# Routing cut into sixteen one-instruction steps, with a new emission order for attention, early table and early weights

## The chip, the cores and the metric

The kernel runs on one NeuronCore of a Trainium2 chip. The metric is the device time of one execution in microseconds (us). Several executions are timed and their median counts. One further execution is recorded by the profiler, and all rows shown here are of that one.

## The reference, cut to what matters

Attention over 8 batches, 8 heads, 576 positions and 64 features is the sum of two parts: one on queries, keys and values averaged over groups of 4, and one in a band of |i-j| < 4. Each token's 8 heads are joined to a row of 512, and the 4608 rows go through a mixture of 8 experts, one expert for each token.

```python
q_d = q.reshape(B, H, Sd, 4, D).mean(axis=3)      # k_d, v_d the same
out_up = np.repeat(sm_attn(q_d, k_d, v_d), 4, axis=2)
scores = np.where(abs(i - j) < 4, scale * q @ k.T, -1e9)
attn = np.exp(scores - scores.max(-1)); attn /= attn.sum(-1) + 1e-9
x = (out_up + attn @ v)  ->  [4608, 512]
...
logits = x @ w_gate + modality_bias[modality_id]
e_idx = np.argmax(logits, axis=1)
gate_w = softmax(logits)[token, e_idx]
for e in range(8):
    h = np.maximum(x[e_idx == e] @ w1[e], 0.0)
    out[e_idx == e] = gate_w[e_idx == e, None] * (h @ w2[e])
```

## The kernel before, in words

**Attention.** The work is cut into 32 units n of two heads each, four units to a batch b. TensorE (PE) transposes q and k (`tp`, `tpt`), multiplies the band in tiles of 24 queries by 32 keys (`sc`, L375) and the averaged part (`scd`, L401). ScalarE (ACT) copies the transposes out (`kT`, `qT`), takes the exponentials of the band (`le`, L392) and of the averaged part (`de`, L414, three to a unit), and copies `Pw`, `PdT`, `vd` and `Od`. VectorE (DVE) takes the maxima (`lm`, `dm`), subtracts (`le`, L387), sums (`z`), inverts (`zr`), transposes (`lt`, L439) and adds both parts to `X` (L490). GpSimd (POOL) averages q (`qe`, `qd`) and divides `le` (L428) and `de` (L432) by their sums. PE then multiplies by v (`avd` L468, `avl` L483). SyncE (SP) issues the loads of q, k and v, the stores of x to the table `xs`, and the weight loads (L851, L854); each of these is one entry in one queue.

**Order.** The order is not left to a scheduler in this part. `PHASE` gives each step a time: step s of unit n is due at n + PHASE[s] (plus ODD[s] for odd n), a routing step of batch b at 4b + PHASE[s]. Further calls with times of their own (loads, early table, early weights) are put on the same list, the list is sorted, and the instructions are emitted in that order. Every engine runs its own instructions in the order of emission, and waits at the first one whose data is not there. So the table decides only who stands behind whom.

**Routing.** For each of the first 6 batches, while attention of later batches runs: PE forms the logits (`lg`, `lgt`), ACT copies them (`LT`), DVE sums them (`L`, L545), adds the bias, finds the maximum and subtracts it (`ch1`, L552 to L555), finds the expert (`ch2`, L566 to L576, `oh` and the running count `acc`), ACT takes the exponential (`ex`, L559), DVE forms the gate (`gt`), PE the place in the expert's list (`pr`, L591 to L595), DVE the slot (`pl`, L603 to L607), and POOL scatters pairs of token and gate to the table `tab` (`st`, L642, up to 5 to a batch). The last two batches are routed after attention.

**Early table and early units.** After 4 batches the counts per expert are taken (`cp`, L654, one PE matmul) and some 25 short DVE instructions (`first`, L657 to L767) find an expert that already has 1024 tokens. Its first 1024 are two early units of 512: SP reads their entries (`tg`), POOL gathers their rows (`xg`, L937, four gathers for the first), SP loads the weights in chunks c (`wload`) and POOL and DVE split each chunk into a high part (CAST, L876) and a low part, raw minus high (`H<-raw`, L882: `wsplit`). The experts' layers (L1005, L1061) follow attention: the early units, then three large units of 1024 tokens and small ones for the rest.

Of the kernel before, what the change touches and what calls it, by code (L numbers as in the profile page):

```python
# [7 lines left out]
F32 = mybir.dt.float32  # L8
# [30 lines left out]
EB = 4  # L39
# [34 lines left out]
}  # L74

ODD = {"Od": 0.0089, "PdT1": 0.0014, "X0": 0.0451, "avd": 0.0124, "avl0": -0.0606, "avl1": -0.068, "de2": 0.0109, "dm": -0.0066, "exp": -0.0422, "kT0": 0.0073, "kT2": -0.0188, "le1": -0.0126, "lm1": -0.0049, "nd": 0.1052, "nl": 0.1593, "pdt0": -0.0317, "qd": 0.0144, "sc0": 0.039, "sc1": -0.0514, "scd": -0.0178, "tpk": -0.005}
# [418 lines left out]
class Router:  # L495
# [65 lines left out]
    def ch2(s, b, i):  # L561

        nc, C, G, L = s.nc, s.C, s.t["G", b], s.t["L", b]
        sh = [128, G, NE]
        w = s.wk.tile(sh, F32, name="w", bufs=1)
        nc.vector.tensor_scalar(w, L, 0.0, None, op0=ALU.is_ge)  # L566
        nc.vector.tensor_tensor(w, w, C.rev.unsqueeze(1).broadcast_to(sh), op=ALU.mult)
        mw = s.wk.tile([128, G], F32, name="mw")
        nc.vector.tensor_reduce(mw, w, op=ALU.max, axis=AX.X)
        oh = s.t["oh", b] = s.wk.tile(sh, BF16, name="oh")  # L570
        nc.vector.tensor_tensor(oh, w, mw.unsqueeze(2).broadcast_to(sh), op=ALU.is_equal)
        s.t["old", b] = s.acc
        an = s.wk.tile([128, NE], F32, name="an")
        nc.vector.tensor_reduce(an, oh.rearrange("p g e -> p e g"), op=ALU.add, axis=AX.X)
        s.acc = s.wk.tile([128, NE], BF16, name="acc")
        s.last_dve = nc.vector.tensor_tensor(s.acc, an, s.t["old", b], op=ALU.add)  # L576

    def gt(s, b, i):

        nc, t0, G = s.nc, s.t["t0", b], s.t["G", b]  # L580
        gt = s.wk.tile([128, G], F32, name="gt")
        nc.vector.tensor_reduce(gt, s.t.pop(("ex", b)), op=ALU.add, axis=AX.X)
        nc.vector.tensor_scalar(gt, gt, 1e-9, None, op0=ALU.add)
        nc.vector.reciprocal(s.C.ig[:, t0 : t0 + G, 1].bitcast(F32), gt)
# [13 lines left out]
    def pl(s, b, i):  # L598

        nc, C, G, t0, oh = s.nc, s.C, s.t["G", b], s.t["t0", b], s.t["oh", b]  # L600
        sh = [128, G, NE]
        sl = s.wk.tile(sh, F32, name="sl", bufs=1)
        nc.vector.tensor_tensor(sl, s.t.pop(("pr", b)), C.ecap.unsqueeze(1).broadcast_to(sh), op=ALU.add)  # L603
        nc.vector.tensor_tensor(sl, sl, oh, op=ALU.mult)
        sf = s.wk.tile([128, G], F32, name="sf")
        nc.vector.tensor_reduce(sf, sl, op=ALU.add, axis=AX.X)
        nc.vector.tensor_copy(C.si[:, t0 : t0 + G], sf)  # L607
# [198 lines left out]
class Moe:  # L806
# [116 lines left out]
    def gather(s, T, n=NTOK + 1, H=2, R=None, h0=0, J=None):  # L923
# [276 lines left out]
def build(tc, q, k, v, mid, w_gate, bias, w1, w2, out):  # L1200
    nc = tc.nc
    with ExitStack() as ctx:
# [10 lines left out]
        with ExitStack() as actx:  # L1213
# [40 lines left out]
            batch = ("lg", "LT", "lgt", "L", "ch1", "ch2", "ex", "gt", "pr", "pl", "st", "R", "W")  # L1254
            for b in range(B):
                call(4 * b + min(P[x] for x in P if x[:2] in ("lg", "R0")), lambda b: ro.begin(b, X[b]), b)
            for nm, p in P.items():
                f, i = (nm[:-1], int(nm[-1])) if nm[-1].isdigit() and nm not in ("ch1", "ch2") else (nm, 0)
# [353 lines left out]
```

## Time and profile before

| what | value |
|---|---|
| three timed executions | 655.83, 656.64, 651.09 us, median 655.83 us |
| the profiled execution | 654.19 us, of it 652.40 us in the profile's span |
| PE, ACT, DVE, POOL busy in the span | 625.1, 383.5, 438.0, 352.1 us |
| TensorE clock granted, mean | 0.99 |
| DMA | 90.21 MB, mean 138 GB/s |

PE is busy for 96% of the span, but this is an average over an attention part of some 246 us and an expert part behind it, and the two have different limits. A view by stretches is needed, and the waits of each engine within a stretch: the time that an engine sat idle at the head of an instruction, and which other instruction ended that.

### The profile page before, as it was taken

The page shows a single profiled execution, that of the slowest core. Times are in us where ns is not written, and L with a number is a line of the kernel's source. Part 1 is how long each engine was busy: PE and PEld are TensorE (multiplying, and loading weights), DVE is VectorE, ACT ScalarE, POOL GpSimd, SP SyncE. Part 2 cuts the span into 40 slices and gives each one's busy share as a digit, 9 for nine tenths or more (in the row PEclk, how much of TensorE's full clock was granted, in tenths as well). Part 3 has the DMA queues.
Part 4 walks back from the last instruction along what each step waited for, and adds up shares of the span by engine and source line. Part 5 has one row for each costly group of instructions (what it writes and reads, how often), then busy time and mean ns, then how long its engine had stood idle before and what let it go on. Part 6 is the DMA issues. An engine that isn't in the chain of part 4 may idle for free. (4 is left out here: it accounts for less than half of the span.)

```text
span 652.4 us, 16389 instructions
## 1 busy us (share of the span) xinstructions
PE 625.1 (96%) x6099; PEld 496.7 (76%) x6099; DVE 438.0 (67%) x880; ACT 383.5 (59%) x858; POOL 352.1 (54%) x406
## 2 busy tenths in 40 slices
PE   8899999988998789999999999999999999999996
PEld 5677777766776556888888888887888878889794
DVE  7789889898987865852456764777647876236610
ACT  4789999987999662322544732447324483346620
POOL 6745765755657870525069775697755720141211
PEclk9999999998999989999999999999999999999998
DMA  7899988999989852597012455133441245549400
GB/s 191 188 181 190 159 163 181 167 208 156 190 157 199 209 191 71 96 225 185 4 45 98 109 130 133 49 98 110 119 144 49 89 112 160 157 130 282 152 23 32
DMA packets 168860, 90.21 MB, mean 138 GB/s; under 512 B 131812, under 2 KB 153354, under 8 KB 168778
## 3 DMA queue, kind: packets, MB, share of 16 engines
q1 hardware_dynamic: 160810, 69.96, 49.9%
q0 software_dynamic: 7968, 19.18, 9.3%
q8 instruction: 49, 0.80, 0.6%
q14 instruction: 33, 0.27, 0.2%
HBM read 69.86 MB, written 19.51 MB: 137 GB/s over the span
## 5 line engine op out<-in xcount | busy, mean ns | idle before, releaser
L1061 PE MATMUL l<-V,H 128*128 128x512 f32 x792 | 184.2, 391 | 0.0
L1061 PEld LDWEIGHTS l<-V,H 128*128 128x128 f32 x792 | 147.9, 188 | 30.6
L945 POOL DMA_INDIRECT xg<-xs,m x64 | 74.1, 1158 | 19.2 <-issue 18.6
L1071 POOL DMA_INDIRECT out_dram<-o,tq x24 | 29.0, 1210 | 76.1 <-ACT o L1063 55.6
L1063 ACT ACTIVATE o<-l,tq 128x512 f32<-128x512 f32 x24 | 16.5, 689 | 68.0 <-PE l L1061 43.1
L1005 PE MATMUL l<-X,H 128*128 128x512 f32 (+1 forms) x240 | 54.5, 376 | 0.0
L642 POOL DMA_INDIRECT tab<-ig,si x36 | 37.0, 1027 | 24.4 <-DVE w L566 15.7
L1005 PEld LDWEIGHTS l<-X,H 128*128 128x128 f32 x240 | 42.0, 190 | 8.1 <-issue 1.0
L1164 ACT ACTIVATE H<-o 128x512 fp32r<-128x512 f32 x36 | 22.8, 634 | 39.2 <-DVE o L1186 39.2
L483 PE MATMUL avl<-Pw,vw 128*64 128x96 f32 x768 | 40.2, 254 | 5.0 <-DVE X L490 1.8
L432 POOL TENSOR_TENSOR de<-de,zr 128x432 f32<-128x432 f32 x32 | 28.9, 904 | 29.7 <-ACT LT L533 13.6
L444 ACT COPY Pw<-lt 32x288 f32<-32x288 f32 x100 | 42.8, 428 | 1.5
L333 ACT COPY kT<-tp 64x512 f32<-64x512 f32 x64 | 37.1, 580 | 8.7 <-PE tp L296 5.7
L483 PEld LDWEIGHTS avl<-Pw,vw 128*64 128x64 f32 x768 | 33.9, 140 | 10.4 <-ACT Pw L444 4.1
L882 DVE TENSOR_TENSOR V<-raw,V 128x1024 fp32r<-128x1024 f32 x22 | 35.2, 1622 | 9.6 <-ACT V L876 9.6
L1071 POOL DMA_INDIRECT out_dram<-o,tg x10 | 11.5, 1154 | 54.0 <-ACT o L1063 41.3
L1011 DVE SCALAR_TENSOR_TENSOR H<-l,H 128x512 fp32r<-128x512 f32 x24 | 16.3, 688 | 34.7 <-ACT H L1010 34.7
L375 PE MATMUL sc<-kT,qT 128*24 128x64 f32 x1536 | 38.5, 223 | 0.3 <-ACT qT L320 0.3
L375 PEld LDWEIGHTS sc<-kT,qT 128*24 128x24 f32 x1536 | 27.5, 103 | 12.1 <-issue 7.5
L414 ACT ACTIVATE de<-scd,dm 128x144 f32<-128x144 f32 x96 | 35.1, 374 | 0.8 <-DVE dm L406 0.5
L401 PE MATMUL scd<-kd,qd 64*64 64x144 f32 x384 | 31.2, 296 | 4.3 <-POOL qd L357 4.3
L1010 ACT ACTIVATE H<-l 128x512 fp32r<-128x512 f32 x24 | 14.2, 597 | 34.9 <-PE l L1005 34.8
(283 smaller groups left out, 1442.3 us busy)
## 6 DMA issues: line engine op xcount, KB each, us to landing
raw<-in_moe_w_dram SPq DMA_DIRECT2D x112, 128.0 KB
raw<-in_moe_w_dram SPq DMA_DIRECT2D x28, 512.0 KB
vw<-in_v_dram SPq DMA_DIRECT2D x60, 180.0 KB
qt<-in_q_dram SPq DMA_DIRECT2D x26, 288.0 KB
kt<-in_k_dram SPq DMA_DIRECT2D x26, 288.0 KB
xs<-R SPq DMA_DIRECT2D x48, 128.0 KB
xs<-G SPq DMA_DIRECT2D x16, 128.0 KB
qt<-in_q_dram SPq DMA_DIRECT2D x6, 256.0 KB
```

Of the source, the lines that this page charges most:

```text
L333: s.nc.scalar.copy(s.kB[r, g, a, PAD + 64 * g : PAD + 64 * g + 512], p[r])
L375: s.nc.tensor.matmul(p[32 * j : 32 * j + SUB, 2 * i : 2 * i + 2, :], qT[:, q0 : q0 + SUB], kB[:, :, q0 : q0 + WIN], start=False, stop=(i = ...
L401: s.nc.tensor.matmul(p[r, c, :], qd[r, 40 * c : 40 * c + 64], kd[r, :], start=True, stop=True, skip_group_check=True)
L414: s.nc.scalar.activation(x, s.t["scd", n][:, c].rearrange("p (k x) -> p k x", k=NB), AF.Exp, bias=m[:, c : c + 1], accum_out=s.t["z", n][: ...
L444: (s.nc.gpsimd.tensor_copy if j in (0,) and n < 28 else s.nc.scalar.copy)(s.Pw[n % NPW][r, :, j, :SUB], s.t["lt", n][r, :, :SUB])
L483: s.nc.tensor.matmul(p[64 * a : 64 * a + 64, c], vw[:, NB * (4 * (hp // 2) + hp % 2 + 2 * a) + k, :], Pw[:, 2 * k + a], start=True, stop=T ...
L642: i = nc.gpsimd.indirect_dma_start(out=s.tab[:, :], out_offset=bass.IndirectOffsetOnAxis(ap=C.si[:, t : t + 1], axis=0), in_=C.ig[:, t, :] ...
L882: (nc.gpsimd if turn == 4 else nc.vector).tensor_tensor(lo, raw, hi.bitcast(F32), op=ALU.subtract)
L945: s.nc.gpsimd.indirect_dma_start(out=R[l].rearrange("p h (i x) -> p (h i) x", i=4)[:, i, :], out_offset=None, in_=s.xs.rearrange("n (a x) ...
L1005: s.mm = nc.tensor.matmul(p[:, f % n, :], a[:, fs], x[:, k, :N], start=(k == 0 and i == 0), stop=(k == 3 and i == 2))
L1061: nc.tensor.matmul(p, l, x[:, f % 2, :], start=(f == 0 and i == 0), stop=(f == 7 and i == (1 if H == 1 else 2)))
L1071: nc.gpsimd.indirect_dma_start(out=s.out[:, :], out_offset=bass.IndirectOffsetOnAxis(ap=T[:, h, 0:1], axis=0), in_=o, in_offset=None, boun ...
```

## The change

The same instructions are computed; what changes is their cutting into steps and their order.

- `ch1`, `ch2`, `gt` and `pl`, four steps of several DVE instructions each, become sixteen steps of one instruction each (`ch0` to `ch8`, `gt0` to `gt2`, `pl0` to `pl3`), each with a time of its own. `EIGHTHS` could put a step on another engine; it is empty, so all stay on DVE.
- `PHASE` and `ODD` get new numbers.
- The pieces of the early table start 0.3 behind `ch8` (at 20.47, before at 19.9) and stand 0.12 apart (before 0.10).
- The last batch's v loads move ahead; the first two weight chunks move from 24.2 and 26.4 to 26.64 and 26.9, behind v. Their splits move from 31.15 and 31.66 to 32.6 and 32.62.
- The last two of the first early unit's four gathers move from 30.64 and 30.66 to 31.76 and 31.77.
- The five scatters of batch 5 leave attention. They are issued on POOL behind the gathers of the second early unit, ahead of the nine of batches 6 and 7.

```diff
-    "dm": 1.5942, "exp": 1.7497, "de2": 1.7635, "z": 1.7851, "de0": 1.8118, "de1": 1.8165,
+    "dm": 1.6155, "exp": 1.765, "de2": 1.7972, "de1": 1.8009, "de0": 1.8118, "z": 2.0454,
...
-    "LT1": 7.1833, "lgt0": 7.4306, "L0": 7.4316, "lgt1": 7.468, "L1": 7.5567, "ch1": 7.5577,
-    "R4": 7.5988, "ch2": 7.6069, "ex": 7.6823, "gt": 7.9472, "W0": 8.0206, "pr": 8.1663,
+    "ch1": 7.6044, "W0": 7.6803, "ch2": 7.7154, "ch3": 7.7531, "ch4": 7.7678, "R4": 7.8666,
+    "ch5": 7.8739, "ex": 7.8853, "ch6": 7.9358, "gt0": 8.1571, "gt1": 8.1581, "ch7": 8.1715,
...
+    def ch(s, b, i):
+
+        nc, C, G, L = s.nc, s.C, s.t["G", b], s.t["L", b]
+        t0, sh, v = s.t["t0", b], [128, G, NE], EIGHTHS.get(("ch", i), "vector")
+        v = getattr(nc, v if b < B - 2 else "vector")
+        if i == 0:
+            v.tensor_tensor(L, L, C.tb[:, t0 : t0 + G, :], op=ALU.add)
+        elif i == 1:
+            s.mx = s.wk.tile([128, G], F32, name="mx")
+            v.tensor_reduce(s.mx, L, op=ALU.max, axis=AX.X)
+        elif i == 2:
+            v.tensor_tensor(L, L, s.mx.unsqueeze(2).broadcast_to(sh), op=ALU.subtract)
...
+        elif i == 4:
+            v.tensor_tensor(s.w, s.w, C.rev.unsqueeze(1).broadcast_to(sh), op=ALU.mult)
...
+        elif i == 6:
+            oh = s.t["oh", b] = s.wk.tile(sh, BF16, name="oh")
+            v.tensor_tensor(oh, s.w, s.mw.unsqueeze(2).broadcast_to(sh), op=ALU.is_equal)
...
+        else:
+            s.t["old", b] = s.acc
+            s.acc = s.wk.tile([128, NE], BF16, name="acc")
+            s.last_dve = v.tensor_tensor(s.acc, s.an, s.t["old", b], op=ALU.add)
...
+        elif i == 1:
+            v.tensor_tensor(s.sl, s.sl, oh, op=ALU.mult)
...
-                    for b in range(B - 2):
+                    for b in range(5 if f == "st" else B - 2):
...
-                        late_ = (1.39, 0.78)[j] if b == B - 2 else 0
+                        late_ = (2.19, 1.06)[j] if b == B - 2 else 0
...
-                call(min(t, 4 * (EB - 1) + P["ch2"] + 0.3) + 0.1 * i, first)
+                call(4 * (EB - 1) + P["ch8"] + 0.3 + 0.12 * i, first)
...
-            for i, x in enumerate((0.64, 1.64, 2.64, 2.66)):
+            for i, x in enumerate((0.64, 1.64, 3.76, 3.77)):
                 call(4 * (B - 1) + x, rows, 0, i)
...
-            for c, x in enumerate((0.2, 2.4, 3.4, 4.4)):
+            for c, x in enumerate((2.64, 2.9, 3.4, 4.4)):
                 call(4 * (B - 2) + x, wload, c)
             for c in range(2):
                 for j in range(2):
-                    call(N - 1 + (0.15, 0.66)[c] + 0.25 * j, wsplit, c)
+                    call(N - 1 + (1.6, 1.62)[c] + 0.46 * j, wsplit, c)
...
+                with tc.issue_after(getattr(moe.fetched, "ins", moe.fetched)):
+                    for b, i in [(b, i) for b in range(5, B - 2) for i in range(5)]:
+                        ro.st(b, i)
```

Line numbers of the changed kernel are higher by 4 before `ch`, and by 18 behind `pl`; so `le` on ACT is L392 before and L396 after, the scatter L642 and L660, the low part L882 and L900. Three places follow, each first before, then after.

ACT around the exponential of the gate, `ex`, of the first batch (`de_166,z` x3 are one unit's three exponentials of the averaged part), before:

```order
L473 ACTIVATE Od<-avd 128x144
L559 ACTIVATE ex<-L 128x32
L392 ACTIVATE le<-le 128x384
L414 ACTIVATE de_166,z<-scd,dm 128x6x24 x3
L461 COPY PdT<-pdt 96x2x144 x2
L333 COPY kT<-tp 64x512 x2
```

ACT at the same place after:

```order
L477 ACTIVATE Od<-avd 128x144
L396 ACTIVATE le<-le 128x384
L418 ACTIVATE de_166,z<-scd,dm 128x6x24 x3
L586 ACTIVATE ex<-L 128x32
L465 COPY PdT<-pdt 96x2x144 x2
L337 COPY kT<-tp 64x512 x2
```

`ex` has moved from ahead of a unit's four exponentials to behind them; the same holds in all six batches that are routed beside attention.

POOL in the last quarter of attention, before (`tab<-ig,si` is a scatter of batch 5, `xg<-xs` a gather of the first early unit, the rest is attention):

```order
L432 TENSOR_TENSOR de_168<-de_168,zr 128x18x24
L642 DMA tab<-ig,si 41472x2
L937 DMA xg<-xs,tg_3850 128x512
L353 TENSOR_TENSOR qe<-qT 128x288
L642 DMA tab<-ig,si 41472x2
L357 TENSOR_TENSOR qd<-qe 128x144
L642 DMA tab<-ig,si 41472x2
L444 COPY Pw_165<-lt 32x12x24
L432 TENSOR_TENSOR de_166<-de_166,zr 128x18x24
L642 DMA tab<-ig,si 41472x2
L937 DMA xg<-xs,tg_3850 128x512
L428 TENSOR_TENSOR le<-le,zr 128x384
```

POOL at the same place after:

```order
L436 TENSOR_TENSOR de_168<-de_168,zr 128x18x24
L955 DMA xg<-xs,tg_3849 128x512
L357 TENSOR_TENSOR qe<-qT 128x288
L361 TENSOR_TENSOR qd<-qe 128x144
L448 COPY Pw_165<-lt 32x12x24
L955 DMA xg<-xs,tg_3849 128x512
L436 TENSOR_TENSOR de_166<-de_166,zr 128x18x24
L432 TENSOR_TENSOR le<-le,zr 128x384
```

The scatters are gone from here, and `qd` follows `qe` at once.

DVE through the last two units, 30 and 31, before (`H<-raw` is the low part of the first two weight chunks, `L423` and `L424` form `zr`):

```order
L347 TENSOR_REDUCE kd<-tp 128x128
L382 TENSOR_REDUCE lm<-sc 128x12
L882 TENSOR_TENSOR H_4731<-raw_3700,H_4731 128x1024
L387 TENSOR_TENSOR le<-sc,lm 128x384
L406 TENSOR_REDUCE dm<-scd 128x3
L439 STREAM_TRANSPOSE lt<-le 128x384
L490 TENSOR_TENSOR X<-avl,Od 128x288 x2
L418 TENSOR_REDUCE z<-le 128x4x3
L882 TENSOR_TENSOR H_4803<-raw_3700,H_4803 128x1024
L423 TENSOR_SCALAR zr<-z 128x15
L424 RECIPROCAL zr<-zr 128x15
```

DVE at the end of unit 31 after:

```order
L410 TENSOR_REDUCE dm<-scd 128x3
L443 STREAM_TRANSPOSE lt<-le 128x384
L494 TENSOR_TENSOR X<-avl,Od 128x288 x2
L422 TENSOR_REDUCE z<-le 128x4x3
L900 TENSOR_TENSOR H_4882<-raw_4060,H_4882 128x1024
L900 TENSOR_TENSOR H_4892<-raw_4060,H_4892 128x1024
L427 TENSOR_SCALAR zr<-z 128x15
L428 RECIPROCAL zr<-zr 128x15
```

The two low parts stood ahead of unit 30's subtraction (`le`, L387) and ahead of its `zr`; now both stand between `z` and `zr` of unit 31, the last one.

## Rows read from the trace of the kernel before

**Rows 1.** Windows: start:end, length, busy (count) PE, PEld, DVE, ACT, POOL, PEclk, DMA, GB/s.

```profile
55.00:134.90 79.90, 78.57 (x1554) 58.59 (x1550) 71.37 (x205) 75.65 (x228) 52.49 (x77) 1.00 0.91 171
134.90:160.00 25.10, 21.13 (x400) 16.25 (x394) 23.06 (x77) 19.46 (x58) 15.02 (x21) 0.93 1.03 172
...
200.00:229.60 29.60, 23.94 (x451) 17.28 (x447) 21.69 (x49) 22.87 (x68) 24.82 (x30) 0.94 1.00 203
...
246.20:636.00 389.80, 389.14 (x1871) 322.47 (x1871) 229.68 (x331) 175.98 (x250) 189.36 (x163) 1.00 0.42 115
```

**Rows 2.** Waits of ACT, 42 to 230 us: releaser, total, times, longest us.

```profile
ACT ex L559 <- DVE L L555: 3.0, 6, 0.6
```

**Rows 3.** Waits of ACT, then of PE, 134.9 to 160 us.

```profile
ACT kT L333 <- PE tp L300: 1.7, 1, 1.7
ACT le L392 <- DVE le L387: 1.7, 1, 1.7
ACT vd L286 <- PE vp L281: 0.7, 1, 0.7
ACT Od L473 <- PE avd L468: 0.5, 1, 0.5
ACT de L414 <- DVE dm L406: 0.5, 1, 0.5
...
PE cp L654 <- DVE X L490: 1.4, 1, 1.4
```

**Rows 4.** Waits of ACT, then of PE and DVE, 200 to 229.6 us.

```profile
ACT vd L286 <- PE vp L281: 2.2, 2, 1.5
ACT Od L473 <- PE avd L468: 1.8, 1, 1.8
ACT le L392 <- DVE le L387: 1.3, 1, 1.3
ACT PdT L461 <- PE tp L300: 0.8, 1, 0.8
...
PE scd L401 <- POOL qd L357: 4.3, 3, 3.0
...
DVE lt L439 <- POOL le L428: 3.9, 1, 3.9
```

**Rows 5.** Timeline of POOL, 196 to 345 us: start, us, instruction, [idle before].

```profile
207.96 1.04 POOL L937 DMA_INDIRECT xg<-xs,tg  x1 [0.30 <-issue]
...
222.15 1.03 POOL L876 CAST H<-raw 128x1024 fp32r<-128x1024 f32 x1
...
261.51 1.03 POOL L642 DMA_INDIRECT tab<-ig,si  x1 [15.67 <-DVE w L566]
```

**Rows 6.** The line of the low parts: ns min/median/max, first to last start.

```profile
L882 DVE TENSOR_TENSOR H<-raw,H x3: 1204/1999/3065, 218.9 to 236.0; 128x1024 fp32r<-128x1024 f32 x3
```

**Rows 7.** Timeline of the last unit's chain, 229.6 to 240 us.

```profile
229.63 0.52 ACT L392 ACTIVATE le<-le 128x384 f32<-128x384 f32 x1
...
232.76 0.83 POOL L428 TENSOR_TENSOR le<-le,zr 128x384 f32<-128x384 f32 x1
...
235.18 0.57 DVE L439 STREAM_TRANSPOSE lt<-le 128x384 f32<-128x384 f32 x1
...
239.59 0.75 PE L483 MATMUL avl<-Pw,vw 128*64 128x96 f32 x6 [1.78 <-DVE X L490]
```

**Rows 8.** Two routing lines with two inputs on DVE, whole span.

```profile
L604 DVE TENSOR_TENSOR sl<-sl,oh x8: 184/192/881, 60.4 to 268.2; 128x32 f32<-128x32 f32 x4, 128x40 f32<-128x40 f32 x4
...
L571 DVE TENSOR_TENSOR oh<-w,mw x8: 191/197/203, 57.2 to 261.9; 128x32 bf16<-128x32 f32 x4, 128x40 bf16<-128x40 f32 x4
```

**Rows 9.** Timeline of SP's queue, 195 to 232 us.

```profile
213.25 0.32 SPq L269 DMA_DIRECT2D vw<-in_v_dram  x1
...
218.22 2.05 SPq L851 DMA_DIRECT2D raw<-in_moe_w_dram  x4
```

More of the change, by code (lines that the diff above doesn't have):

```diff
@@ L61 @@
 PHASE = {
[12 rows of a table removed]
-}
-ODD = {"Od": 0.0089, "PdT1": 0.0014, "X0": 0.0451, "avd": 0.0124, "avl0": -0.0606, "avl1": -0.068, "de2": 0.0109, "dm": -0.0066, "exp": -0.0422, "kT0": 0.0073, "kT2": -0.0188, "le1": -0.0126, "lm1": -0.0049, "nd": 0.1052, "nl": 0.1593, "pdt0": -0.0317, "qd": 0.0144, "sc0": 0.039, "sc1": -0.0514, "scd": -0.0178, "tpk": -0.005}
[14 rows of a table added]
+}
+ODD = {"Od": 0.0007, "PdT0": 0.0299, "PdT1": 0.0514, "X0": -0.0168, "X1": -0.0025, "avd": 0.0233, "avl0": -0.0369, "avl1": -0.068, "de0": 0.0067, "de2": 0.0919, "dm": 0.058, "exp": -0.0312, "kT0": 0.0601, "kT2": 0.0135, "le1": -0.0126, "lm1": 0.0097, "mk0": 0.0135, "nd": 0.0476, "nl": 0.1046, "pdt0": -0.0186, "qT0": 0.02, "qd": -0.0132, "qe": 0.0472, "sc0": 0.0678, "sc1": -0.0514, "scd": 0.0099, "tpk": -0.0019, "tpq": 0.0009, "z": -0.2805, "zr": -0.1893}
+EIGHTHS = {}
 def whole(pieces):
@@ L559, in ex @@
         s.last_act = s.nc.scalar.activation(ex, s.t["L", b], AF.Exp)
[L561 to L576, printed above, removed]
     def gt(s, b, i):
         nc, t0, G = s.nc, s.t["t0", b], s.t["G", b]
[L581 to L584, printed above, removed]
+        v = getattr(nc, EIGHTHS.get(("gt", i), "vector") if b < B - 2 else "vector")
+        if i == 0:
+            s.sum = s.wk.tile([128, G], F32, name="gt")
+            v.tensor_reduce(s.sum, s.t.pop(("ex", b)), op=ALU.add, axis=AX.X)
+        elif i == 1:
+            v.tensor_scalar(s.sum, s.sum, 1e-9, None, op0=ALU.add)
+        else:
+            v.reciprocal(s.C.ig[:, t0 : t0 + G, 1].bitcast(F32), s.sum)
     def pr(s, b, i):
@@ L600, in pl @@
         nc, C, G, t0, oh = s.nc, s.C, s.t["G", b], s.t["t0", b], s.t["oh", b]
[L601 to L607, printed above, removed]
+        sh, v = [128, G, NE], getattr(nc, EIGHTHS.get(("pl", i), "vector") if b < B - 2 else "vector")
+        if i == 0:
+            s.sl = s.wk.tile(sh, F32, name="sl", bufs=1)
+            v.tensor_tensor(s.sl, s.t.pop(("pr", b)), C.ecap.unsqueeze(1).broadcast_to(sh), op=ALU.add)
+        elif i == 1:
+            v.tensor_tensor(s.sl, s.sl, oh, op=ALU.mult)
+        elif i == 2:
+            s.sf = s.wk.tile([128, G], F32, name="sf")
+            v.tensor_reduce(s.sf, s.sl, op=ALU.add, axis=AX.X)
+        else:
+            v.tensor_copy(C.si[:, t0 : t0 + G], s.sf)
     def st(s, b, t):
@@ L936, in gather @@
         for h in range(h0, H):
-            nc.gpsimd.indirect_dma_start(
+            s.fetched = nc.gpsimd.indirect_dma_start(
                 out=R[:, h, :], out_offset=None, in_=s.xs[:n, :],
@@ L1253, in build @@
             used = max(P["avl0"], P["avl1"])
-            batch = ("lg", "LT", "lgt", "L", "ch1", "ch2", "ex", "gt", "pr", "pl", "st", "R", "W")
+            batch = ("lg", "LT", "lgt", "L", "ch", "ex", "gt", "pr", "pl", "st", "R", "W")
             for b in range(B):
@@ L1257, in build @@
             for nm, p in P.items():
-                f, i = (nm[:-1], int(nm[-1])) if nm[-1].isdigit() and nm not in ("ch1", "ch2") else (nm, 0)
+                f, i = (nm[:-1], int(nm[-1])) if nm[-1].isdigit() else (nm, 0)
                 if f in batch:
-                    for b in range(B - 2):
+                    for b in range(5 if f == "st" else B - 2):
                         call(4 * b + p, getattr(ro, parts.get(f, f)), b, i)
@@ L1379, in build @@
                             f(b, i)
-                for f in (ro.ch1, ro.ex):
-                    for b in last:
-                        f(b, 0)
                 for b in last:
-                    ro.ch2(b, 0)
-                    ro.gt(b, 0)
+                    for i in range(3):
+                        ro.ch(b, i)
+                for b in last:
+                    ro.ex(b, 0)
+                for b in last:
+                    for i in range(3, 9):
+                        ro.ch(b, i)
+                    for i in range(3):
+                        ro.gt(b, i)
                     if b == B - 1:
@@ L1388, in build @@
                     ro.pr(b, 0)
-                    ro.pl(b, 0)
+                    for i in range(4):
+                        ro.pl(b, i)
                     for i in range(5):
```

17 lines of the change are left out of this document (10 added, 7 removed), and 20 rows, old and new, of the table PHASE.

## The prediction

> **What bounds the kernel now.** I read the busy times by stretches first. From 246.2 to 636 us PE is busy for 389.14 of 389.80 us at full clock [rows 1]: the expert part is bound by its matmuls, whose number the change leaves alone, so it can only start earlier or later. In attention another engine sets the pace. From 55 to 134.9 us ACT is busy for 75.65 of 79.90 us and PE for 78.57; ACT's rows there stand end to end, while PE's busy time is that of many small matmuls whose waits the profile counts as pipelined work. I take ACT as the bound, since over 42 to 230 us its waits are few and each has a name. So the gain lies in those waits and in the tail after the last exponential of unit 31, which starts at 229.63 us [rows 7]. The next view is therefore ACT's waits, and from there what the releaser itself waited for. Two stretches stand out. In 134.9 to 160 us, where the early table is worked out, ACT is busy for 19.46 of 25.10 us only; in 200 to 229.6 us, where scatters, gathers and the first weight chunks come, for 22.87 of 29.60 [rows 1].
>
> **The routing pieces.** In each of the 6 batches `ex` makes ACT wait for DVE's subtraction, 3.0 us in all, at most 0.6 each [rows 2]. After the change `ex` stands behind a unit's four exponentials, that is some 1.6 us of ACT work (0.52 for `le` [rows 7] and three `de` of about as much together with their sums), more than the longest wait. But DVE's subtraction is itself cut off from the two instructions ahead of it, and other work of DVE now stands between; half of the 3.0 can come back. Bounds: a gain of 0 and of 3.0. I take **-1.5**: one of the six lies in the early-table stretch, whose DVE is fullest, and a wait of ACT for DVE elsewhere is the row nearest to it. The instructions themselves are the same ones, so their sum costs nothing more if their durations stay. Six of a batch's sixteen read two inputs from memory. Line L604 is such a one, and once took 0.881 us against 0.192 in the median, while POOL divided `le`; but L571, of the same kind, never took over 0.203 in eight batches [rows 8]. The Trainium skill ("GPSIMD Engine Reference", section 8, Key points) says that GpSimd shares its memory interfaces with VectorE and that DVE instructions with two inputs there contend with it; L604's longest agrees, L571's eight do not show it. By the rows the sum gets nothing for it; by that sentence, if every such piece fell beside POOL, it is the second rival.
>
> **The early table.** ACT's named waits in this stretch, besides `ex`, are 1.7 + 1.7 + 0.7 + 0.5 + 0.5 = 5.1 us [rows 3]. The first 1.7 (`kT` for PE's transposes) has PE behind it, which held at the count matmul `cp` for 1.4 us, for a buffer that DVE's `X` had not freed [rows 3]. After the change `cp` stands behind a block of `sc` and ahead of `avd`, no longer ahead of the transposes that feed `kT`, so I take the 1.7 as gone; `avd` is what is late next if `cp` waits again. The other 3.4 are waits for DVE or for PE behind DVE, and there DVE is the filled one: busy 23.06 of 25.10 us, 92%, against 71.37 of 79.90, 89%, in the stretch before [rows 1]. The pieces are spread from 0.10 to 0.12 of a unit apart and begin 0.57 of a unit later, so that the same work has 20% more room; but the pieces of routing still stand around them. I take 1.3 of 3.4, bounds 0 and 3.4. Sum **-3.0**, bounds 0 and -5.1. Nothing waits for the table's end, since its early entries are read only four units later.
>
> **The late stretch.** ACT's waits are 2.2 + 1.8 + 1.3 + 0.8 = 6.1 us [rows 4]. Their roots stand in the same group: PE held at `scd` for POOL's `qd` for 4.3 us, 3.0 of it at once, and DVE held at `lt` for POOL's `le` for 3.9 us. POOL is busy for 24.82 of 29.60 us here, the fullest it is anywhere in attention [rows 1]. The change takes five scatters of about 1.03 us each and two gathers of 1.04 out of this stretch [rows 5], 5 x 1.03 + 2 x 1.04 = 7.2 us, so `qd` follows `qe` at once, and both roots should go. The low parts of two weight chunks, 1.2 and 2.0 us [rows 6], also leave the path to `le` of unit 30. What is late next is ACT itself. I take 85%, **-5.2**, bounds -2.0 (only the longest wait's 3.0 gone, 1.0 of it given back elsewhere) and -6.1. The scatters cost nothing where they go: POOL sits idle for 15.67 us ahead of the first late scatter [rows 5], waiting for routing on DVE, and five scatters of 1.03, 5.2 us, fit there. If that cover failed, 5.2 us would fall on the lists of the later units, which PE doesn't reach for tens of us. On SP the v loads pass ahead of x stores and weights. The last v part before was issued at 213.25 us and the next weights at 218.22 [rows 9]; the two early chunks now queue behind v, so the second lands about when the third did. That is a price of the tail.
>
> **The tail.** From `le` of unit 31 (229.63) it is 9.96 us to the last but one group of `avl` at 239.59 [rows 7]. Between `z` and `zr` of that unit stand two low parts of 2.0 us (the median [rows 6]), 4.0 us, on the path: `zr`, POOL's `le`, `lt`, `Pw`, `avl`. Against it stands cover: POOL's `le` is done at 232.76 + 0.83 = 233.59 and `lt` starts only at 235.18, 1.6 us later, since DVE was busy with other work; and the 1.78 us that PE waited ahead of `avl` for an `X` standing behind a low part of 3.06 us [rows 6, 7] goes, because both `X` stand ahead of it now. So 4.0 - 1.6 - 1.8 = **+0.6**. Bounds: low parts of 1.2 each give 2.4 - 3.4 = -1.0; of 3.06 each, 6.1 - 3.4 = +2.7. If the chunk lands late the low parts wait in order and all behind them do too; that is the first rival.
>
> **Waits that the new order adds elsewhere.** DVE now takes `lm` ahead of `kd` in all units, and PE `avd` ahead of `scd` in odd ones; no row shows what these cost. The nearest rows are single waits of ACT for such steps, 0.5 to 1.8 us [rows 3, 4]. They could as well gain that much. I take **+1.0**, bounds -1.8 and +1.8.
>
> **The sum.** -1.5 - 3.0 - 5.2 + 0.6 + 1.0 = -8.1 us. The profiled execution took 654.19 us, 1.64 below the median of the three timed ones and near the mean of all four; 654.19 - 8.1 = **646.1 us**.
>
> **Rivals.** *First: the tail or the table gives the gain back*, about 651 us. The order decides that the last unit's `zr` waits for two weight chunks, and with it everything behind. If the second chunk's low part starts 2 to 3 us late, or takes 3.06 us like the last one, the tail costs 2.7 + 2 instead of 0.6, and the sum is -4.0: 650.2. The same comes out if the early table gives nothing (+3.0) with one us more of new waits: 650.1, since DVE at 92% is the bound there and spreading does not lessen its work. Here the change would not do what it says. For it: low parts from 1.2 to 3.06 us in one kernel; against it: the row nearest to the second chunk's new place is the issue at 218.22 [rows 9], and the forecast has that `z` some 3 us later, so that a wait is short. Its times are 649.5 to 655.
>
> *Second: routing becomes slower on DVE*. Of 6 x 6 = 36 instructions with two inputs, one of the six of L604 showed 0.881 instead of 0.192, +0.69. Standing alone among attention's steps, each may fall beside a POOL instruction: with 30 more so stretched, 30 x 0.69 = 20.7 us. DVE's idle time, 8.53 of 79.90 us [rows 1], is some 16.5 us over the 155 us in which routing runs, and half of it, 8.3, can take that up. So 646.1 + 12.4 = 658.5 us, slower than before; it decides from (8.1 + 8.3) / 30 = 0.55 us for each. Against it stands L571 with 0.203 at most [rows 8]. Its times are 655 to 665.
>
> *Third: more is gained.* All of 3.0, 5.1 and 6.1 goes, the tail gives -1.0 and the new order as much as it costs, 0: -15.2, 639 us; two thirds of the excess is about 641.
>
> **Chances.** Forecast (643 to 649.5) 0.53; first rival 0.25; second 0.10; third 0.12. A change of about 1% is what a measurement of this kernel can tell from none, so the marks are 649.3 and 662.4 around 655.83. Faster by over 1%: nearly all of the forecast, and the third, with little of the first: 0.62. Within 1%: 0.31, most of the first and two thirds of the second. Slower: 0.07. The range reaches into the third and through most of the first: 640.5 to 656.5.
>
> **What the changed profile would show.** Right: ACT's waits in 200 to 230 us under 2 us, none of PE for `qd` over 1; the exponential of unit 31 at 220 to 222 us; `ex` waits under 2 us in sum; five scatters ahead of the 15 us idle stretch of POOL; the first stretch of saturated PE from about 238 instead of 246. Wrong: ACT still at 19 to 20 busy of 25 us in the table's stretch; a low part that waits for the weights between `z` and `zr` of unit 31; routing lines on DVE with medians over 0.3 us; or an expert part longer than 390 us, which nothing here would explain.

## The result, and the profile after

| | before | changed |
|---|---|---|
| median of 20 executions | 655.6 us | 648.91 us |
| ratio, 95% interval | | 0.9886 (0.9866 to 0.9905) |
| profiled execution, its span | 654.19, 652.40 us | 647.43, 645.74 us |

The forecast was 646.1 us, with a range of 640.5 to 656.5. By the ratio the change is worth 1.1%, some 7.5 us of 655.6; by the profiled executions 6.8 us. The single executions of one kernel scatter from 644.8 to 653.2, and that scatter turned out to belong to the question.

The windows of the changed kernel, columns as in [rows 1]:

```profile
55.00:134.90 79.90, 76.47 (x1502) 57.53 (x1504) 66.81 (x199) 75.01 (x222) 51.28 (x74) 1.00 0.90 169
134.90:160.00 25.10, 23.55 (x460) 17.49 (x457) 23.60 (x83) 22.61 (x70) 15.50 (x22) 1.00 0.87 177
160.00:200.00 40.00, 36.82 (x692) 27.55 (x689) 32.38 (x101) 34.35 (x102) 21.30 (x32) 0.96 1.03 172
200.00:229.60 29.60, 26.00 (x511) 19.99 (x509) 23.97 (x56) 27.90 (x85) 19.13 (x27) 1.00 0.92 227
...
246.20:636.00 389.80, 388.97 (x1851) 323.97 (x1850) 227.53 (x327) 173.77 (x246) 192.90 (x167) 1.00 0.42 114
```

ACT, the engine that paces attention, is busy for 22.61 of 25.10 us around the early table and 27.90 of 29.60 in the late stretch, against 19.46 and 22.87 before [rows 1]; the changed kernel's attention ends inside that last stretch, so the two are not quite the same work. GpSimd has fallen from 24.82 to 19.13 there. Only the stretch from 160 to 200 us is emptier than one would wish; I come back to it. The waits that answer to [rows 3] (ACT, then PE) are these:

```profile
ACT PdT L465 <- PE pdt L457: 0.8, 1, 0.8
ACT vd L290 <- PE vp L285: 0.5, 1, 0.5
ACT le L396 <- DVE le L391: 0.3, 1, 0.3
ACT de L418 <- DVE eo L720: 0.2, 1, 0.2
ACT de L418 <- DVE dm L410: 0.2, 1, 0.2
...
PE cp L672 <- DVE acc L582: 0.3, 1, 0.3
```

and those that answer to [rows 4] (ACT, then DVE; PE has none for `qd`):

```profile
ACT kT L337 <- PE tp L304: 0.5, 1, 0.5
ACT PdT L465 <- PE pdt L457: 0.3, 1, 0.3
...
DVE lt L443 <- POOL le L432: 1.0, 1, 1.0
```

5.1 us of waits have become 2.0, and 6.1 have become 0.8. The count matmul `cp` waits 0.3 us instead of 1.4.

A clock of its own for attention is the start of ACT's exponential of the band, once for each unit (L392 before, L396 after). The last rows mark where the expert matmuls begin to run without a pause, and the end. Three traces of the changed kernel stand here, the second and third taken beside the experiments, on two chips:

| stretch, in us | before | changed | second | third |
|---|---|---|---|---|
| start to unit 4 | 42.73 | 40.40 | 40.15 | 40.11 |
| unit 4 to 18 | 92.22 | 93.83 | 91.04 | 92.05 |
| 18 to 22, early table | 31.49 | 27.96 | 27.80 | 32.95 |
| 22 to 28 | 39.25 | 43.98 | 41.32 | 40.48 |
| 28 to 31, late | 23.94 | 17.96 | 18.48 | 21.20 |
| 31 to pauseless experts | 13.62 | 11.83 | 12.79 | 11.78 |
| from there to the end | 409.19 | 409.78 | 410.05 | 409.68 |

In the first trace the two stretches on which the forecast rested gave 3.5 and 6.0 us. Two that it had left out count as well: the first four units gave 2.3, and units 22 to 28 took 4.7 back in the first trace and 2.1 in the second. The second trace is the quietest: 641.63 us in its span, 10.8 less than before. Of the kernel before there is one trace only, so every difference in this table leans on it.

### The profile page after: what moved, and what is told of

Read it like the earlier page. It is cut to its first block, busy times and chain, and to the rows that moved or that the text cites. A ratio compares the mean times of both kernels' runs of the same rounds, so it can differ in the third digit from the quotient of the medians.

```text
span 645.7 us, 16349 instructions
## 1 busy us (share of the span) xinstructions
PE 622.8 (96%) x6099; PEld 496.1 (77%) x6099; DVE 426.8 (66%) x880; ACT 385.1 (60%) x858; POOL 351.1 (54%) x406
## 5 line engine op out<-in xcount | busy, mean ns | idle before, releaser
L963 POOL DMA_INDIRECT xg<-xs,m x64 | 76.7, 1198 | 19.2 <-issue 19.2
L1089 POOL DMA_INDIRECT out_dram<-o,tq x24 | 27.7, 1153 | 74.8 <-ACT o L1081 52.6
L1023 PE MATMUL l<-X,H 128*128 128x512 f32 (+1 forms) x240 | 54.2, 374 | 0.0
L1023 PEld LDWEIGHTS l<-X,H 128*128 128x128 f32 x240 | 41.5, 189 | 8.0 <-issue 0.8
L660 POOL DMA_INDIRECT tab<-ig,si x36 | 36.0, 1000 | 15.7 <-issue 6.9
L432 POOL TENSOR_TENSOR le<-le,zr 128x384 f32<-128x384 f32 x32 | 26.6, 831 | 28.8 <-DVE si L625 22.1
L900 DVE TENSOR_TENSOR V<-raw,V 128x1024 fp32r<-128x1024 f32 x22 | 35.2, 1625 | 9.6 <-ACT V L894 8.9
L1143 DVE TENSOR_TENSOR G<-X,G 128x1024 fp32r<-128x1024 f32 x15 | 23.3, 1551 | 21.4 <-ACT G L1142 21.2
```

The source lines that it names most:

```text
L660: i = nc.gpsimd.indirect_dma_start(out=s.tab[:, :], out_offset=bass.IndirectOffsetOnAxis(ap=C.si[:, t : t + 1], axis=0), in_=C.ig[:, t, :] ...
L900: (nc.gpsimd if turn == 4 else nc.vector).tensor_tensor(lo, raw, hi.bitcast(F32), op=ALU.subtract)
L963: s.nc.gpsimd.indirect_dma_start(out=R[l].rearrange("p h (i x) -> p (h i) x", i=4)[:, i, :], out_offset=None, in_=s.xs.rearrange("n (a x) ...
L1023: s.mm = nc.tensor.matmul(p[:, f % n, :], a[:, fs], x[:, k, :N], start=(k == 0 and i == 0), stop=(k == 3 and i == 2))
L1089: nc.gpsimd.indirect_dma_start(out=s.out[:, :], out_offset=bass.IndirectOffsetOnAxis(ap=T[:, h, 0:1], axis=0), in_=o, in_offset=None, boun ...
```

## The experiments

Times are compared with the kernel before, on the same chip. The edits below are to the changed kernel.

**The changed kernel again.**

> The changed kernel once more, with nothing edited. In its first trace everything stood still from 177.2 to 179.5 us and the interval from the exponential of unit 24 to that of unit 25 was 10.0 us, against 6.8 in the kernel before. Theory: that stop belongs to this order, so it is there again at unit 24 (8.5 us or more) and the time is 649 again, 6.7 us below before. Rival: it fell there by chance, so the interval is 6.5 to 7.2 us and the time of the profiled execution is about 3 us lower, 644 to 645.

Measured: 645.12 us, before 653.8, ratio 0.984 (0.9798 to 0.9882). The interval from unit 24 to 25 was 8.2 us, between the two expectations: the stop of 2.2 us in the first trace is not there, but 1.4 us more than the 6.8 of before remain. They have a wait of PE beside them, ahead of the matmul that averages v (`vp`) for unit 24:

```profile
178.81 0.85 PE L285 MATMUL vp<-vw,pool 128*32 128x256 f32 x9 [1.65 <-ACT Od L477]
```

The profile names ACT's `Od`, but the last part of v had landed at 178.56 us, 0.25 us before this start; I come to that under the third trace.

**All late edits undone.**

```diff
-range(5 if f == "st" else B - 2)   (and the five scatters behind the gathers)
+range(B - 2)
-late_ = (2.19, 1.06)[j]
+late_ = (1.39, 0.78)[j]
-(0.64, 1.64, 3.76, 3.77)
+(0.64, 1.64, 2.64, 2.66)
-wload (2.64, 2.9, ...), wsplit (1.6, 1.62)[c] + 0.46 * j
+wload (0.2, 2.4, ...), wsplit (0.15, 0.66)[c] + 0.25 * j
```

The early experts' number is also read 1.1 units earlier, which the early loads need.

> The changed kernel with all edits of the late part that are not in the tables undone: batch 5's scatters beside attention, the early gathers, v loads, first two weight loads and their splits at their old times. Theory: the late part is worth 5 us here, mostly through GpSimd; the time is 653 to 655, 1 to 3 below before, PE waits for qd and DVE for le on GpSimd again (3 to 4 us each after 200 us). Rival: the new tables alone carry the gain, and the time is 648 to 650.

Measured: 652.62 us, ratio 0.9986 (0.9955 to 1.0016): the gain is gone. From unit 28 to 31 it took 26.41 us, against 18.48 in the changed kernel on this chip. The waits on GpSimd are back, and one of PE for v of the last batch (PE, PE, DVE; 202 to 232 us, and 200 to 232 for the last):

```profile
PE scd L405 <- POOL qd L361: 2.6, 1, 2.6
PE vp L285 <- DMA vw<-in_v_dram: 2.1, 1, 2.1
...
DVE lt L443 <- POOL le L432: 2.2, 1, 2.2
```

**The old tables.**

```diff
-PHASE, ODD of the changed kernel
+PHASE, ODD of the kernel before (ch0..2 at ch1, ch3..8 at ch2, gt0..2 at gt, pl0..3 at pl)
```

> The changed kernel with the tables PHASE and ODD of the kernel before (the pieces of a routing step all at their step's old time), all other edits kept. Theory: the late part's gain stays, 5 us, and what the table gave at the gate's exponential and at the count matmul, about 3 us, goes: 650 to 651.5. Rival: the gain is the tables'; 655 to 656, and the exponential of unit 31 starts within 1.5 us of 229.6.

Measured: 647.88 us, ratio 0.9898 (0.9871 to 0.9926). Units 28 to 31 took 17.7 us and 18 to 22 took 29.1, 2.4 less than before with nothing but the distance of 0.12 changed there. The rival fell, and the theory's 650 to 651.5 missed too, on the other side: the late edits alone carry 5.9 of the 8.7 us on this chip, and the whole new table, with its sixteen steps, adds 2.8 by the medians of six executions each. The intervals of the two ratios just overlap, so that the 2.8 is not firm. The 2.4 rests on one trace of each kernel.

**The early table's pieces at their old places.**

```diff
-call(4 * (EB - 1) + P["ch8"] + 0.3 + 0.12 * i, first)
+call(4 * (EB - 1) + 7.6069 + 0.3 + 0.1 * i, first)
```

> The changed kernel with only the early table's pieces at their old start (19.9) and distance (0.10). Theory: the spreading gave some 1.3 us of the early stretch's gain; ACT is busy for about 21 of the 25.1 us from 134.9, and the time is 650 to 651. Rival: the count matmul's new place behind the band scores gave it all, or nothing in the stretch hangs on the distance: ACT busy for 22.3 us or more there and 648.5 to 649.5. Second rival: it is the whole of the stretch's 3.5 us: ACT busy for 19.5 us, 652 to 653.

Measured: 856.89 us. This is no price of a wait. With `ch8` now later, the count matmul came before the count of the fourth batch was added (PE's line, then DVE's):

```profile
133.09 0.18 PE L672 MATMUL cp<-acc,ones 128*128 128x8 bf16 x1
...
135.65 0.17 DVE L582 TENSOR_TENSOR acc<-an,acc 128x8 bf16<-128x8 f32 x1
```

In the changed kernel `acc` is at 138.54 and `cp` at 138.76. I read it so: with three batches counted no expert is sure of 1024 tokens, the early units carry nothing, and other units do their work later; the first layer's matmuls of this form on L1023 number 480 against 240:

```profile
L1023 PE MATMUL l<-X,H 128*128 128x256 f32 (+1 forms) x480 | 92.3, 337 | 0.0
```

So the later start is no tuning: the pieces' new times need it. All three expectations missed.

**The old distance alone.**

```diff
-... + 0.3 + 0.12 * i, first)
+... + 0.3 + 0.1 * i, first)
```

> The changed kernel with only the distance of the early table's pieces at 0.10 again, the start kept behind ch8 (the run that also put the start back let the count be taken a batch too early, which changed the experts' work, and said nothing of the time). Theory: up to the exponential of unit 22 the two differ by 0.5 to 1.5 us, and the time is 0.5 to 1.5 above the changed kernel's. Rival: nothing hangs on the distance, 0.0 to 0.4.

Measured: 650.74 us, before 661.7 on this chip, ratio 0.9859 (0.9792 to 0.9925). Beside 0.984 to 0.9886 of the changed kernel no loss can be told, but six executions could not tell 0.5 to 1.5 us from none. The trace bounds it better: units 18 to 22 took 30.24 us with a wait of 1.85 us ahead of `vp` at unit 20, and 29.82 in the run with the late edits undone, which has the new distance and a wait of 1.96 at the same place. So with the new table the distance is worth some 0.4 us there by these two traces, at the border of theory and rival, and is not what gives the early stretch its gain.

**The parts of the late edits, one at a time**, each undone as in the diff above.

> The changed kernel with only batch 5's five scatters back beside attention. The late edits together were worth 7.5 us (652.6 without them, 645.1 with them, same chip). Theory: GpSimd is the root of the late waits, so the scatters carry more than half: the time is 4 to 5 us above the changed kernel's on this chip, PE waits for qd and DVE for le on GpSimd for 2 us or more after 200 us. Rival: the low parts of the weight chunks carry it; within 1.5 us of the changed kernel.

Measured: 660.92 us, ratio 0.9924 (0.9861 to 0.9987).

> The changed kernel with the v loads, the first two weight loads and their splits at their old times (and the early experts' number read 1.1 units earlier, which those loads need). Theory: some 2 us above the changed kernel: one low part of 1.2 to 2.0 us stands ahead of unit 30's subtraction again, and the pair between z and zr of unit 31 goes. Rival: the low parts and v carry the late gain: 5 us or more above, with a wait of PE for v of 2 us as in the run with all late edits undone.

Measured: 657.25 us, ratio 0.9971 (0.9932 to 1.0011).

> The changed kernel with only the last two of the first early unit's gathers back at 30.64 and 30.66. Theory: two gathers of 1.04 us each on a GpSimd that has room since the scatters left: 0 to 1 us above the changed kernel. Rival: any GpSimd work there is on the path: 2 us above.

Measured: 659.56 us, ratio 0.9984 (0.9943 to 1.0026).

On this chip the kernel before took 654.5 to 672.1 us, and the unedited changed kernel was not run on it, so the medians rank the three only roughly. The traces help. With the low parts back, units 28 to 31 took 22.9 us and the tail 14.2; against 18.48 and 12.79 of the second trace that is 5.8 us, more than the 2 expected. It is mostly not the low parts: from unit 29 to 31 that run lost 0.6 us, and the rest has loads beside it, which this edit puts behind the weights again. PE waited for k of unit 29:

```profile
PE tp L304 <- DMA kt<-in_k_dram: 2.6, 1, 2.6
```

and 1.0 us ahead of `vp`. So the rival came nearer, with k in the place of v. With the gathers back, 28 to 31 took 18.8 us, as in the changed kernel: that trace lost its time between units 22 and 26, where PE waited 4.0 us for v. Nothing in it speaks against the gathers' new place; why the median is as high as with all late edits undone (0.9984 and 0.9986) stays open. With the scatters back 28 to 31 took 23.5 us, but the trace shows a second cause, GpSimd's gather at the head of its queue:

```profile
203.65 1.09 POOL L955 DMA_INDIRECT xg<-xs,tg  x1 [4.79 <-issue]
205.04 1.04 POOL L660 DMA_INDIRECT tab<-ig,si  x1 [0.31 <-issue]
206.11 0.67 POOL L357 TENSOR_TENSOR qe<-qT 128x288 f32<-128x288 f32 x1
206.95 0.98 POOL L660 DMA_INDIRECT tab<-ig,si  x1 [0.16 <-issue]
207.96 0.43 POOL L361 TENSOR_TENSOR qd<-qe 128x144 f32<-128x144 f32 x1
```

PE waited 5.1 us for that `qd`. The changed kernel's third trace has a gather delayed by 4.85 us too, without scatters behind it, and took 21.20 us from unit 28 to 31. The difference, 2.3 us, is about the two scatters ahead of `qd`, 1.04 + 0.98; it is an estimate from one trace each, on two chips.

**v earlier.**

```diff
-late_ = (2.19, 1.06)[j] if b == B - 2 else 0
+late_ = (2.19, 1.06)[j] if b == B - 2 else (0, 0.45)[j]
```

> The changed kernel with the second half of every batch's v loads (but the last batch's, which the change moved) 0.45 of a unit earlier, so that SP issues it ahead of the q and k loads and of the x store that the new table put in front of it. In two traces of the changed order PE waited 2.2 and 4.0 us for v at unit 24, and in the undisturbed one v landed only some 0.3 us ahead of its use. Theory: this store ahead of v is why units 23 to 25 give 2 us back, or more on a chip whose transfers land later; they come back, and the time is 1 to 4 us below the changed kernel's of the same chip, with no wait of PE for v. Rival: v is early enough in most executions and q and k are now late instead: no difference within 1 us, or worse.

Measured: 650.4 us, ratio 0.9876 (0.9821 to 0.9931), beside 649.84 of the unedited kernel. The theory's remedy fell. PE waited 4.0 us for v, now at unit 16. I had moved the wrong half: the half that units 16, 20 and 24 wait for is the first one, and with the second issued right behind it the first's last part took 10.4 us to land in this trace.

**The changed kernel a third time, on that chip.**

> The changed kernel unedited, for comparison on this chip. Both theories: 0.983 to 0.990 of the kernel before. Theory of late v: the interval from the exponential of unit 24 to 25 is above 8 us where v lands later than 10 us after its issue, and near 8.2 otherwise; rival: it has no relation to v.

Measured: 649.84 us, ratio 0.9876 (0.9825 to 0.9928). In this trace the large wait for v is at unit 20, not 24, and the interval from unit 24 to 25 was 6.96 us, below both expectations (PE, then SP's queue):

```profile
155.39 1.43 PE L285 MATMUL vp<-vw,pool 128*32 128x256 f32 x9 [3.52 <-DMA vw<-in_v_dram]
```

```profile
139.01 3.82 SPq L654 DMA_DIRECT2D xs<-R  x4
142.88 4.66 SPq L273 DMA_DIRECT2D vw<-in_v_dram  x4
```

SP issues four x stores (L654) and only then v. From the last issue, at 144.84, v took 10.4 us to land; in the second trace 7.0, and PE did not wait. From the landing of the last v part to its use I find 4.1, 8.4 and 4.0 us at units 16, 20 and 24 before, and 0.2, 1.3 and 0.7, then 0.3, 1.2 and 0.2, then 0.1, 0.1 and 0.3 in the three traces of the changed kernel. The slack is gone in all of them, and where it ran out PE stood. Over all traces PE's idle time just ahead of `vp` of unit 24 goes with the interval from unit 24 to 25:

| trace | PE idle ahead of `vp`, us | unit 24 to 25, us |
|---|---|---|
| before, old tables, old routing | 0 | 6.81, 6.81, 6.95 |
| changed, third | 0.01 | 6.96 |
| scatters back, v earlier | 0.76, 1.02 | 7.66, 7.58 |
| low parts back, late edits undone | 1.52, 1.53 | 8.45, 8.09 |
| changed, second; early table's old places | 1.65, 1.85 | 8.21, 8.41 |
| old distance, old start, gathers back | 2.17, 3.62, 4.01 | 9.12, 11.34, 11.80 |
| changed, first (with its own stop) | 0 | 10.03 |

The profile puts these waits down to v in some traces and to ACT's `Od`, `kT` or `Pw` in others, but in all nine with 0.7 us or more the last part of v had landed 0.25 us (once 0.34) before `vp` began, whatever ACT was doing. So the wait is v's, and it comes with the new times of routing and x stores: the three traces with the old ones have none.

**The old routing.**

```diff
-routing steps and x stores (lg ... W) at the new times
+the same steps at the times of the kernel before, pieces of a step together
```

> The changed kernel with the routing steps (and the x stores) at the times of the kernel before, the pieces of each step together and ex ahead of the unit's exponentials again; attention's steps and all late edits as changed. Theory: the sixteen pieces are worth the six waits of ACT for the subtraction, 1.5 to 3 us, which show in ACT's waits for ex again; 1.5 to 3 us above the changed kernel. Rival: those waits are taken up elsewhere and v passes the stores again, which gives 2 us: within 1 us of the changed kernel or below it.

Measured: 650.41 us, ratio 0.9885 (0.9827 to 0.9942), as the unedited kernel. Its waits of ACT, 42 to 200 us, show both halves of the trade: no wait for v any more, and instead

```profile
ACT de L424 <- DVE dm L416: 8.2, 7, 1.7
ACT ex L592 <- DVE L L570: 5.0, 6, 1.4
```

so `ex` waits again, six times. With the stores behind v, v lands 7.1 and 6.1 us ahead of its use at units 20 and 24 again (0.7 at 16). So both halves of the rival are in the trace, `ex` waiting and v in time. But the medians cannot weigh them: 0.6 us between six executions that scatter over 3.1 and 6.5 us tells neither 1.5 us nor nothing. Nor does the trace, whose execution took 654.0 us: from unit 17 to 18 it has a stop of its own, 12.17 us against 6.34 in the second trace (PE idle for 2.46 us with no wait shown, then the granted clock at 0.50). That the pieces' gain and the late v cancel is likely, and not shown.

**The old start.**

```diff
+p_, odd = (OLD[nm], OLD_ODD) if n < 3 else (p, ODD)
```

> The changed kernel with attention's steps of units 0 to 2 at the times of the kernel before. The undisturbed trace of the changed kernel is 2.6 us ahead by unit 4, which the prediction had not counted. Theory: the order of the first units alone makes this: the exponential of unit 4 starts within 0.5 us of 42.7 and the time is 2.6 us above the changed kernel's. Rival: it comes from the order of units 3 and 4 as well, and 1 us or less is lost.

Measured: 651.76 us, ratio 0.9872 (0.9813 to 0.993). The trace confirms the place: unit 4 is at 43.85 us, 3.7 later than in the unedited kernel on this chip (expected were 42.7 us and 2.6 later), and with the old tables whole it was at 44.13. But 1.9 us in the medians (651.76 against 649.84) is within their scatter, so the size rests on the trace alone.

## Why the prediction was right, point by point

The sum held better than its terms. The bound and the roots of the late waits were right. But the start and the clock in the tail gave some 4 us that no term had, and units 4 to 28 took back up to 6.3; that this cancels to within 1.4 us of the forecast is partly luck. By the medians on one chip the late edits are worth 7.5 us with the new tables and 5.9 with the old, and the tables 2.8 and 1.2 us; only the first two stand clear of the scatter.

**The bound** was read rightly: the expert part took 409.2 to 410.1 us in all four traces, and the gain came from stretches in which ACT had named waits.

**Late stretch** (-5.2): measured -6.0, -5.5 and -2.7 from unit 28 to 31; with the late edits undone the whole gain was lost. The root was named rightly in part. The scatters on GpSimd are one share (2.3 us by the traces), the places of the k, v and weight loads with the low parts another (5.8 us with the tail), which I had priced as a by-product. The spread has its cause in a step that I had costed at nothing: the early entries `tg`, which the gathers need, come later. They were issued at 193.25 us before and landed with 4 us to spare ahead of the gather at 200.62; in the changed kernel at 197.16, and the gather waited:

```profile
201.11 1.09 POOL L955 DMA_INDIRECT xg<-xs,tg  x1 [1.00 <-PE avl L487]
```

In all three traces it begins 1.06 us after the first of the entries landed (200.05, 196.07, 202.80 us), and PE's wait for `qd` behind it was 0, 1.4 and 2.8 us. The new place of v alone is not the reason: with v and the weights at their old times the gather waits too (1.49 and 1.51 us), and with the old tables, v in its new place, it does not (0.16). So the new table has a part in it; which step is not shown.

**Scatters' new place** (nothing): right. The five run from 243.99 to 250.15 us, and GpSimd still idles for 5.72 us behind them:

```profile
243.99 1.04 POOL L660 DMA_INDIRECT tab<-ig,si  x1 [0.30 <-issue]
...
255.88 0.97 POOL L660 DMA_INDIRECT tab<-ig,si  x1 [5.72 <-DVE w L569]
```

**Early table** (-3.0): -3.5 and -3.7 in the first two traces; in the third a wait for v hides it. Against the run with the old tables on the second trace's chip it is only 1.3. `cp` behaved as forecast. That 1.3 of it comes from the distance was not shown: with the old tables the distance alone gave 2.4, with the new one nothing that can be told.

**`ex`** (-1.5): its waits are gone from ACT's list between 42 and 230 us, against 3.0 [rows 2], and 5.0 come back when the routing is put back. From unit 4 to 18 the second trace gained 1.2 us, and two runs whose order is the same up to there gained 1.0 and 1.2 (late edits undone, early table's old places); that is the new table as a whole, and the share of `ex` is not shown apart. Part of its waits moved: ACT's `de` for DVE's `dm` waited 0.5 us before and 1.8, 2.0 and 3.8 in the three traces. The first trace lost 1.6 instead: PE stood for 1.1 us ahead of `vp` at unit 16, whose v had landed 0.14 us before, and the rest I could not trace to an engine.

**Tail** (+0.6): by the prediction's own measure, from `le` to that `avl`, it was 9.64, 10.60 and 9.59 us against 9.96, so -0.3, +0.6 and -0.4. The term of 4.0 us for two low parts was too high: the pair ran in 2.34 us, 1.21 each, and GpSimd was idle beside it; the 2.00 and 3.06 us of before had GpSimd's divisions or its own low part beside them. The other error cancels it: 1.26 of the 1.78 us ahead of `avl` stayed, now for `Pw`. The chain of unit 31 (exponential, low parts, GpSimd, `lt`, `avl`):

```profile
224.13 0.52 ACT L396 ACTIVATE le<-le 128x384 f32<-128x384 f32 x1
...
226.03 2.34 DVE L900 TENSOR_TENSOR H<-raw,H 128x1024 fp32r<-128x1024 f32 x2
...
228.91 0.91 POOL L436 TENSOR_TENSOR de<-de,zr 128x432 f32<-128x432 f32 x1 [3.10 <-DVE zr L428]
229.77 0.83 POOL L432 TENSOR_TENSOR le<-le,zr 128x384 f32<-128x384 f32 x1
...
230.64 0.58 DVE L443 STREAM_TRANSPOSE lt<-le 128x384 f32<-128x384 f32 x1 [0.67 <-POOL le L432]
...
233.77 0.72 PE L487 MATMUL avl<-Pw,vw 128*64 128x96 f32 x12 [1.26 <-ACT Pw L448]
```

The `lt` that stood idle behind other work before now waits for GpSimd's `le` itself, so the cover of 1.6 us was used as forecast. The first rival (the chunk lands late) did not come. The table above gives the tail 1.8, 0.8 and 1.8 us, because some 1.5 lies behind that `avl`: the same matmuls, two groups of `avl` and three of the first layer between them, ran at a granted clock of 0.54 before and at 1.00 in the changed kernel (before, then changed):

```profile
237.80:239.60 1.80, 0.02 (x4) 0.04 (x2) 1.80 (x3) 1.75 (x5) 1.80 (x2) 0.98 0.00 0
239.60:243.25 3.65, 3.65 (x27) 2.57 (x27) 1.49 (x3) 2.22 (x4) 2.77 (x4) 0.54 0.67 249
...
232.50:233.77 1.27, 0.01 (x2) 0.01 (x1) 1.27 (x2) 1.22 (x4) 1.19 (x2) 1.00 1.05 395
233.77:235.96 2.19, 2.19 (x28) 1.54 (x28) 1.53 (x3) 1.80 (x3) 2.19 (x2) 1.00 0.23 87
```

PE had stood for 1.78 us before that stretch in the one and for 1.26 in the other. The prediction had no term for the clock.

**New waits elsewhere** (+1.0): wrong in its parts, and its size was luck. The start gave 2.3 to 2.6 us, which I had not looked for, and units 4 to 28 together took back between 0.9 us (the second trace) and 6.3 (the first), early table left out; net that is +4.0, -1.7 and -1.6 in the three traces. The part of it that I can name is v behind the x stores: 1.1 us of PE's time at unit 16 in the first trace, 1.65 at unit 24 in the second, 5.2 at units 16, 20 and 26 in the third. I had gone through SP's queue for the last batch only; in every batch the stores passed ahead of v.

**The second rival** (routing slower beside GpSimd) fell: L604's line, now L620, has 200 ns as its longest, and L571's, now L575, 224. The piece that is stretched most often, the addition of the bias, is so more rarely than before (before, then changed, then L620):

```profile
L552 DVE TENSOR_TENSOR L<-L,tb x8: 192/347/393, 55.3 to 260.5; 128x32 f32<-128x32 f32 x4, 128x40 f32<-128x40 f32 x4
...
L559 DVE TENSOR_TENSOR L<-L,tb x8: 157/196/389, 53.2 to 254.7; 128x32 f32<-128x32 f32 x4, 128x40 f32<-128x40 f32 x4
...
L620 DVE TENSOR_TENSOR sl<-sl,oh x8: 182/193/200, 57.6 to 262.3; 128x32 f32<-128x32 f32 x4, 128x40 f32<-128x40 f32 x4
```

The sentence of the Trainium skill on shared interfaces ("GPSIMD Engine Reference", section 8, Key points) is borne out in part. L552 is a piece with two inputs, and in five of its six times beside attention it ran beside GpSimd's `qd` and took 347 to 393 ns; the low parts are another case, 1.21 us with GpSimd idle and 3.06 beside its own low part. Not every overlap costs: other pieces took 191 to 201 ns beside GpSimd. The prediction took L571's 0.203 as evidence against it, but no time that L571 ran beside attention lay beside an instruction of GpSimd, so it could show nothing, and neither can L620 and L575 now. The rival fell because of where the new order puts the pieces, and not because such pieces cannot be stretched.

**What stays open** is the stop of PE in the first trace, 177.2 to 179.5 us: its results came late with no wait shown, all engines stood behind it, and in the second and third traces it is not there; the run with the old routing has one like it at another unit, so it need not belong to this order. Nor was v's first half tried earlier, or the stores behind it with the sixteen steps kept, which the traces point to. Of the signs that the prediction had set, the waits of ACT after 200 us stayed under 2 us in the first two traces (0.8 each) and not in the third (3.6); PE's for `qd` stayed under 1 in the first alone; and the exponential of unit 31, forecast at 220 to 222 us, came at 224.13, 218.79 and 226.79: the forecast knew neither the start's gain nor v's wait.

## What to carry to other kernels

Where one engine paces a pipeline, add up its named waits by stretch and follow each to what its releaser waited for: that gave the size of this change within 1.5 us, with terms that missed by more and cancelled. A reordering that looks free on the engines may be paid in the queue that issues the loads: measure, for every load that something passes, how long before its use it landed, for all iterations and not the last alone. And when one computed step moves later, check what was timed against it: a count taken too early cost some 210 us, and attention showed nothing of it (unit 31 at 219.09 us, as in the second trace); the cost stood in the expert part, where PE waited 75.4 us for gathered rows and had more matmuls to do. And where the profile names a different releaser for one wait in each trace, see which input landed at the same distance before the start in all of them.

## What was not expected of the hardware

The same order took 641.6 to 648.3 us of span in three traces. Part of the difference is landing time: the four v loads for unit 20, issued within 2.0 to 2.5 us, landed 4.6 to 7.0 us after their issue in the second trace and 8.3 to 10.4 in the third. Behind PE's stop in the first trace its granted clock fell to 0.50, that is 1.2 of 2.4 GHz, in the window from 182 to 184 us:

```profile
177.20:179.40 2.20, 1.12 (x17) 0.71 (x13) 0.46 (x1) 0.54 (x4) 1.70 (x3) 1.00 0.94 166
179.40:180.20 0.80, 0.07 (x1) 0.07 (x2) 0.69 (x2) 0.52 (x2) 0.00 (x0) 1.00 1.05 181
180.20:182.00 1.80, 1.80 (x32) 1.30 (x34) 0.65 (x3) 1.75 (x5) 0.86 (x2) 0.64 1.21 156
182.00:184.00 2.00, 2.00 (x16) 1.60 (x18) 1.62 (x3) 1.91 (x7) 1.88 (x3) 0.50 1.29 118
```

So a stall of PE can be paid twice, by its standing and by a lower clock behind it. Here the second part is not shown to cost time, since ACT, which paces attention, is busy for 1.75 of 1.80 and 1.91 of 2.00 us in those windows. In the tail it did: the matmuls at 0.54 took 3.65 us and the same ones at 1.00 took 2.19.
